# Top-k attention with a leaky-ReLU MLP on one core: earlier reciprocals, one TensorE transpose for each hurried pair of units, and a new chunk's MLP behind the exponentials

## The chip, the cores and the metric

The kernel runs on one core of a Trainium2 chip. A core has a matrix engine (TensorE, PE in the profile), a vector engine (VectorE, DVE), an engine for activations and copies (ScalarE, ACT), a general engine (GpSimd, POOL), a sync engine (SyncE, SP) that issues transfers, and 16 DMA engines. Each engine works through its own queue and waits for the others by semaphores. The metric is the time of one execution on the device in microseconds.

## The reference

What must be computed, cut to the core. Attention has 8 batches of 8 heads, 576 tokens and a head width of 64; the MLP works on the 4608 tokens at width 512, with 2048 hidden units.

```python
scores = scale * np.matmul(q, k.transpose(0, 1, 3, 2))
kth = np.partition(scores, -32, axis=-1)[..., -32:-31]
scores = np.where(scores >= kth, scores, -1000000000.0)
scores = scores - np.max(scores, axis=-1, keepdims=True)
attn = np.exp(scores)
attn = attn / (np.sum(attn, axis=-1, keepdims=True) + 1e-09)
attn_out = np.matmul(attn, v)
x = attn_out.transpose(0, 2, 1, 3).reshape(B * S, H * D)      # 4608 x 512
h = x @ w_in                                                   # 512 -> 2048
out = np.maximum(0.01 * h, h) @ w_out                          # 2048 -> 512
```

## The kernel before

**Units.** Attention is cut into 144 units. A unit holds 128 rows of queries of a pair of heads, so two score matrices of 128 x 576 (`both`). Where 64 rows are left over at the end of a sequence, a unit takes 64 rows of two pairs of heads. Four units in a row fill the width of 512 for their tokens.

**The steps of a unit.** `scores` multiplies queries and keys on TensorE for two units at once and ScalarE copies the result out of PSUM (L210, L217). `top_k` takes four rounds on VectorE: it first orders the two halves of each row into pairs (L240), then takes eight largest values (L245) and removes them (L248) in each of the four rounds. The first two rounds read 288 values, the last two 576. `mask` pushes all values below the 32nd down, on GpSimd (L258, L259). `exponents` and `sums` are on ScalarE (L262, L267): the result of `sums` is `ze`. `reciprocals` on VectorE makes `rz` of it (L271), and `normalize` multiplies with it on ScalarE (L274). Then the weights are transposed so that they can multiply the values (`weigh_values`, L318, on TensorE); `keep_values` copies the result into `x` of the chunk on ScalarE (L332).

**Two ways to transpose.** `transpose` splits the 32-bit words into two halves of 16 bits on ScalarE (L283), writes them to DRAM and has a DMA transposition read them back into `wT` (L286). `transpose_in_haste` does nine 128 x 128 transpositions on TensorE into two PSUM tiles named `wide` (L296) and copies these on ScalarE (L297). There are two `wide` tiles in all, and the scores and the weighted values use them too.

**Chunks.** The tokens are cut into 19 chunks: two of 128 and 17 of 256. A chunk's MLP can start when all of its units are weighted. `mlp` is a generator that does a few matmuls at each step: L343, L348, L353, L354 and L381 in the first two chunks, L369, L375 and L381 in the others; L388 copies the result out.

**The order.** It is written out by hand. There is one stage for each unit, and each engine gets its work in the order of the program. In stage s, VectorE does top k of unit s, GpSimd masks unit s-1, ScalarE exponentiates unit s-1, and unit s-2 is normalized and transposed. Every second stage computes the scores of two units ahead. `slot()` emits the next round of top k, and `mlp_steps(budget)` emits MLP matmuls, seven times in each stage; `slot_budget` spreads the backlog over the stages until the next chunk is complete.

**Hurried pairs.** `values_at` says in which stage a pair of units is weighted: the two units 2m and 2m+1 in stage 2m+4. Where the second of a pair completes one of the early chunks (units 3, 7, 15, 23 and 31: `HURRIED`), it is one stage earlier, at 2m+3, and both units of the pair are transposed on TensorE: the first at the end of stage 2m+2, the second at the start of stage 2m+3. There the reciprocals and the normalization come ahead of top k, and `values(s)` behind the first MLP slot. The chunk's MLP can then fill the six other slots of that stage.

Of the kernel before, what the change touches and what calls it, by code (L numbers as in the profile page):

```python
# [8 lines left out]
F32 = mybir.dt.float32  # L9
# [6 lines left out]
NKC = 5  # L16
# [3 lines left out]
def kernel(  # L20
# [14 lines left out]
    NPAIR, P, S = qT.shape  # L35
# [26 lines left out]
    work = ctx.enter_context(tc.tile_pool(name="work", bufs=2))  # L62
# [92 lines left out]
    def load_qk(pi):  # L155
        qt = loads.tile([P, S], F32, name="qt")
        kt = loads.tile([P, S], F32, name="kt")
        nc.sync.dma_start(qt, qT[pi])
        nc.sync.dma_start(kt, kT[pi])
        qk_of[pi] = qt, kt  # L160
# [108 lines left out]
    def reciprocals(u):  # L269
        u.rz = small.tile([P, 2], F32, name="rz")  # L270
        nc.vector.reciprocal(u.rz, u.ze)  # L271

    def normalize(u, i):
        nc.scalar.activation(u.s[i], u.s[i], AF.Copy, bias=0.0, scale=u.rz[:, i:i + 1])  # L274

    def transpose(u):


        pairs = u.both.rearrange("p i n -> p (i n)").bitcast(U16).rearrange("p (n h) -> p n h", h=2)
        apart = halves.tile([P, 2, 2 * S], U16, name="apart")  # L280
        for h in range(2):
            split = work.tile([P, 2 * S], U16, name="split", bufs=2)
            nc.scalar.copy(split, pairs[:, :, h])  # L283
            nc.sync.dma_start(apart[:, h, :], split)
        u.wT = work.tile([P, 2 * NKC - 1, P], F32, name="wT", bufs=3)
        nc.sync.dma_start_transpose(out=u.wT.bitcast(U16), in_=apart.rearrange("p h n -> (p h) n"))  # L286

    def transpose_in_haste(u):

        u.wT = work.tile([P, 2 * NKC - 1, P], F32, name="wT", bufs=3)  # L290
        both = u.both.rearrange("p i n -> p (i n)")
        for c0, c1 in ((0, 8), (8, 2 * NKC - 1)):
            pt = ps_sc.tile([P, 2, 512], F32, name="wide", bufs=2)
            pt = pt.rearrange("p h (c n) -> p (h c) n", n=P)
            for c in range(c0, c1):
                nc.tensor.transpose(pt[:, c - c0, :], both[:, c * P:(c + 1) * P], ident)  # L296
            nc.scalar.copy(u.wT[:, c0:c1, :], pt[:, 0:c1 - c0, :])  # L297


# [57 lines left out]
    def mlp(ch):  # L357

        n = CHUNKS[ch]
        t0 = sum(CHUNKS[:ch])  # L360
        x = x_of[ch]
        if ch < EARLY:
            yield from hidden_of_few(x)
        for f0 in range(0, NFC if ch >= EARLY else 0, 2):
            ph = ps_ml.tile([P, 2, CHMAX], F32, name="ph", tag="ml")
            for i in range(2):
                f = f0 + i
                for c in range(HP):
                    nc.tensor.matmul(  # L369
                        ph[:, i, 0:n], w_in[c][:, f * P:(f + 1) * P], x[c][:, 0:n],  # L370
                        start=(c == 0), stop=(c == HP - 1),
                    )
                    if c == 1 or i == 0 and c == HP - 1:
                        yield 2 * max(n, 225)
            nc.scalar.activation(gT[:, f0:f0 + 2, 0:n], ph[:, :, 0:n], AF.Prelu, alpha=SLOPE)  # L375
            yield 2 * max(n, 225)
        for r0 in range(0, n, P):
            m = min(P, n - r0)
            pz = ps_ml.tile([P, 512], F32, name="pz", tag="ml")
            for f in range(NFC):  # L380
                nc.tensor.matmul(  # L381
                    pz[0:m, 0:DMODEL], gT[:, f, r0:r0 + m], w_out[f // 4][:, f % 4, :],
                    start=(f == 0), stop=(f == NFC - 1),
                )
                if f % 2 and f + 1 < NFC:
                    yield 2 * DMODEL
            o_sb = work.tile([P, DMODEL], F32, name="o_sb", bufs=1)
            nc.scalar.copy(o_sb[0:m], pz[0:m, 0:DMODEL])  # L388
            nc.sync.dma_start(out[t0 + r0:t0 + r0 + m, :], o_sb[0:m])
            yield 2 * DMODEL  # L390
# [10 lines left out]
    def mlp_steps(budget):  # L401
        owed[0] += budget
        while owed[0] > 0:
            if running[0] is None:
                if not ready:
                    owed[0] = 0.0
                    return
                running[0] = mlp(ready.pop(0))
            cost = next(running[0], None)
            if cost is None:  # L410
                running[0] = None
            else:
                owed[0] -= cost
                backlog[0] -= cost
# [5 lines left out]
    HURRIED = {3, 7, 15, 23, 31}  # L420
# [24 lines left out]
    def slot_budget(s):  # L445

        after = [at for at, _ in ready_at if at >= s]
        until = after[0] if after else s
        few = len(after) >= len(CHUNKS) - EARLY
        return backlog[0] / (max(until + 1 - few - s, 1) * SLOTS)  # L450
# [3 lines left out]
    with tc.manual_schedule():  # L454
        last = {p: n for n, u in enumerate(steps) for p in u.pairs}

        def load_more(s):

            for of, load, n, lag in ((qk_of, load_qk, LOADED, -2), (v_of, load_v, LOADED_V, LAG + 1)):
                while len(of) < NPAIR and (len(of) < n or last[len(of) - n] + lag <= s):  # L460
                    load(len(of))


        for n in range(3):
            load_weights(n)
        rounding = {}
        for n in range(NPIECE + 2):
            for i in (n, n - 1, n - 2) if AS_WORDS else ():
                if 0 <= i < NPIECE:
                    if i == n:  # L470
                        rounding[i] = round_weights(i)
                    next(rounding[i], None)
            load_weights(n + 3)
            if 6 <= n < 6 + HP:
                load_qk(n - 6)
            elif n == NPIECE - 3:
                first_scores(steps[0])
            elif n == NPIECE:
                first_scores(steps[1])
            if n == NPIECE - 1:  # L480
                load_v(0)
                load_v(1)

        def values(s):
            due = [u for n, u in enumerate(steps) if values_at(n) == s]
            if due:
                po = ps_sc.tile([P, 2, 512], F32, name="wide", bufs=2)[:, 0, 0:2 * P]
                po = po.rearrange("p (u n) -> p u n", u=2)
            for part in (weigh_values, keep_values):
                for n, u in enumerate(due):  # L490
                    part(u, po[:, n, :])
            attended(s)

        for s in range(len(steps) + LAG + 1):
            cur, old, older, new = unit(s), unit(s - 1), unit(s - 2), ()
            if s % 2 == 0:
                new = [u for u in steps[s + 2:s + 4] if u]
            picks = top_k(cur) if cur else iter(())
            budget = slot_budget(s)

            def slot():
                next(picks, None)

            if s - 2 in HURRIED:
                reciprocals(older)
                normalize(older, 0)
                normalize(older, 1)
                transpose_in_haste(older)
                older = None
            slot()  # L510
            if old:
                mask(old, 0)
                mask(old, 1)
            mlp_steps(budget)
            if s - 2 in HURRIED:
                values(s)
                budget = slot_budget(s + 1)
            slot()
            if older:
                reciprocals(older)  # L520
                normalize(older, 0)
                normalize(older, 1)
            mlp_steps(budget)
            if old:
                exponents(old, 0)
            if older and s - 1 not in HURRIED:
                transpose(older)
            slot()
            mlp_steps(budget)
            mlp_steps(budget)  # L530
            slot()
            mlp_steps(budget)
            if old:
                exponents(old, 1)
                sums(old)
            if s - 1 in HURRIED:
                transpose_in_haste(older)
            if new and s < HURRY:
                scores(new)
            if s % 2 == 0:  # L540
                values(s)
            if new and s >= HURRY:
                scores(new)
            budget = slot_budget(s + 1)
            mlp_steps(budget)
            mlp_steps(budget)
            load_more(s)
        mlp_steps(1e9)
# [58 lines left out]
```

## Time and profile before

The median of three runs is 1501.92 us (1501.92 to 1502.21). The profiled execution spans 1500.9 us.

| Engine | Busy us | Share of the span | Main work |
|---|---|---|---|
| TensorE | 1405.3 | 94% | L381 509.5 us, L369 481.1 us |
| VectorE | 1328.8 | 89% | L245 635.6 us, L248 459.8 us, L240 213.7 us |
| ScalarE | 1091.2 | 73% | L283 293.8 us, L262 221.1 us, L274 207.0 us |
| GpSimd | 1097.8 | 73% | L258 638.3 us, L259 406.9 us |

A share of the span is an average: the first 75 us round the weights and load the first queries and keys, the last 55 us or so hold only the last chunk's MLP, and the stages in between are limited by different engines. A group of instructions has its line, its engine, the tile that it writes and those that it reads, its count, its busy time with the mean of one in ns, and the idle time of the engine just before it with what ended it. The chain of waits ran 31% of the span through L381, 26% through L369 and 10% through L318. The transpositions on TensorE are 90 instructions (L296), and the DMA transpositions 134.

### The profile page before, as it was taken

To read this page: it belongs to the slowest core of one execution; us is meant where nothing else is said; L and a number is where in the kernel's file an instruction comes from. 1 tells how busy PE (TensorE), PEld (TensorE's weight loads), DVE (VectorE), ACT (ScalarE), POOL (GpSimd) and SP (SyncE) were. 2 spreads that over 40 slices of the span, in tenths; PEclk is the share of its full clock that TensorE was granted. 3 is DMA by queue.
4 is the path that set the end of the run, shared out by engine and by line. 5 is a ranking of instruction groups with operands and counts; after the bars stand their busy time and mean duration, and the time that the engine had idled before them with its cause. 6 is when DMAs were issued, how large, how long until landed. Compare 5 with 4: busy or idle time off the path is not lost.

```text
span 1500.9 us, 24188 instructions
## 1 busy us (share of the span) xinstructions
PE 1405.3 (94%) x8122; PEld 934.6 (62%) x8122; DVE 1328.8 (89%) x3414; ACT 1091.2 (73%) x1979; POOL 1097.8 (73%) x742
## 2 busy tenths in 40 slices
PE   6709878999999999999999999999999999999999
PEld 2305446667575757575757676767676766666774
DVE  7997898979999999999999999999999999999600
ACT  8646676858688878787878787878787877777720
POOL 2286787868788887878878888777888888788700
PEclk9959989999999999999999999999999999999999
DMA  8621263624456455645664566555655555555510
GB/s 331 239 63 37 68 159 93 170 63 130 136 147 172 127 162 169 178 132 161 172 174 135 141 158 174 163 145 141 193 151 158 140 156 161 164 130 141 137 52 14
DMA packets 373053, 215.24 MB, mean 143 GB/s; under 512 B 319680, under 2 KB 319680, under 8 KB 370880
## 3 DMA queue, kind: packets, MB, share of 16 engines
q1 hardware_dynamic: 372928, 213.69, 50.5%
q8 instruction: 64, 1.05, 0.3%
q14 instruction: 61, 0.50, 0.1%
HBM read 46.14 MB, written 88.47 MB: 90 GB/s over the span
## 4 chain that ended last, share of the span: by engine, by line
PE 79%; DVE 8%; DMA 6%; ACT 5%; POOL 1%; issue 1%; SPq 0%; DVEq 0%; POOLq 0%; ACTq 0%
PE pz L381 31%; PE ph L369 26%; PE wide L318 10%; PE wide L210 6%; DMA wT<-apart 3%; PE narrow L210 3%; DVE tops L245 2%; DMA apart<-split 2%; ACT split L283 2%; DVE pairs L248 2%; ACT s_sb L274 1%; ACT s_sb L262 1%; PE ph L343 1%; ACT wT L297 1%; DVE w_out L149 1%
## 5 line engine op out<-in xcount | busy, mean ns | idle before, releaser
L258 POOL TENSOR_SCALAR pen<-s_sb,tops 128x576 f32<-128x576 f32 x288 | 638.3, 2216 | 233.6 <-DVE tops L245 201.9
L245 DVE MAX8 tops<-pairs 128x8 f32<-128x288 f32 (+1 forms) x1152 | 635.6, 591 | 0.0
L381 PE MATMUL pz<-w_out,gT 128*128 128x512 f32 x1152 | 509.5, 597 | 4.0 <-ACT gT L354 4.0
L369 PE MATMUL ph<-x,w_in 128*128 128x256 f32 x2176 | 481.1, 381 | 0.0
L248 DVE MATCH_REPLACE8 pairs<-tops,pairs 128x288 f32<-128x288 f32 (+1 forms) x864 | 459.8, 537 | 0.0
L369 PEld LDWEIGHTS ph<-x,w_in 128*128 128x128 f32 x2176 | 410.7, 190 | 77.1 <-issue 23.4
L259 POOL TENSOR_TENSOR s_sb<-s_sb,pen 128x576 f32<-128x576 f32 x288 | 406.9, 1413 | 24.0
L381 PEld LDWEIGHTS pz<-w_out,gT 128*128 128x128 f32 x1152 | 216.2, 190 | 271.0 <-issue 265.9
L283 ACT COPY split<-s_sb 128x1152 uint16<-128x1152 uint16 x268 | 293.8, 1145 | 0.0
L274 ACT ACTIVATE s_sb<-s_sb,rz 128x576 f32<-128x576 f32 x288 | 207.0, 769 | 38.9 <-DVE rz L271 38.8
L262 ACT ACTIVATE s_sb<-s_sb,nbias 128x576 f32<-128x576 f32 x288 | 221.1, 768 | 11.5 <-POOL s_sb L259 11.2
L240 DVE TENSOR_TENSOR pairs<-s_sb 128x576 f32<-128x576 f32 x288 | 213.7, 780 | 9.8
L318 PEld LDWEIGHTS wide<-wT,vt 128*64 128x64 f32 x3200 | 158.9, 138 | 57.3 <-ACT ze L267 17.4
L318 PE MATMUL wide<-wT,vt 128*64 128x128 f32 (+1 forms) x3200 | 178.1, 266 | 16.8 <-ACT wT L297 6.9
L375 ACT ACTIVATE gT<-ph 128x512 f32<-128x512 f32 x136 | 80.8, 594 | 79.4 <-PE ph L369 79.4
L332 ACT COPY x<-wide 128x128 f32<-128x128 f32 (+1 forms) x160 | 32.2, 260 | 142.2 <-PE wide L318 142.2
L217 ACT COPY s_sb<-wide 128x704 f32<-128x704 f32 x142 | 107.1, 754 | 24.3 <-PE wide L210 24.2
L210 PE MATMUL wide<-kt,qt 64*128 64x352 f32 (+1 forms) x632 | 117.1, 490 | 5.1 <-ACT wT L297 4.4
L271 DVE RECIPROCAL rz<-ze 128x2 f32<-128x2 f32 x144 | 22.4, 155 | 70.5 <-ACT ze L267 70.4
L217 ACT COPY s_sb<-narrow 128x448 f32<-128x448 f32 x142 | 68.7, 536 | 2.2 <-PE narrow L210 1.5
L388 ACT COPY o_sb<-pz 128x512 f32<-128x512 f32 x36 | 21.1, 586 | 64.1 <-PE pz L381 64.1
L210 PE MATMUL narrow<-kt,qt 64*128 64x224 f32 (+1 forms) x632 | 67.5, 358 | 0.0
(58 smaller groups left out, 596.1 us busy)
## 6 DMA issues: line engine op xcount, KB each, us to landing
apart<-split SPq DMA_DIRECT2D x268, 288.0 KB, 2.1
raw<-in_weights_dram SPq DMA_DIRECT2D x16, 1024.0 KB, 6.9
vt<-in_vk_dram SPq DMA_DIRECT2D x32, 320.0 KB, 3.5
qt<-in_qT_dram SPq DMA_DIRECT2D x32, 288.0 KB, 3.6
kt<-in_kT_dram SPq DMA_DIRECT2D x32, 288.0 KB, 3.9
out_dram<-o_sb SPq DMA_DIRECT2D x36, 256.0 KB, 2.0
wT<-apart SPq DMA_TRANSPOSE x134, 4.6
```

Of the source, the lines that this page charges most:

```text
L210: nc.tensor.matmul(to[r0:r0 + u.rows, i, :], qt[d, u.q0:u.q0 + u.rows], kt[d, k0:k1], start=True, stop=True)
L240: nc.vector.tensor_tensor(pairs[:, :, n, :], u.both[:, :, 0:HS], u.both[:, :, HS:S], op)
L245: nc.vector.max(out=u.tops[:, i, r, :], in_=rest[i])
L248: nc.vector.match_replace(out=rest[i], in_to_replace=u.tops[:, i, r, :], in_values=rest[i], imm_value=LOWEST)
L258: nc.gpsimd.tensor_scalar(pen, u.s[i], u.tops[:, i, ROUNDS - 1, 7:8], MASKED, ALU.is_lt, ALU.mult)
L259: nc.gpsimd.tensor_tensor(u.s[i], u.s[i], pen, ALU.add)
L262: nc.scalar.activation(u.s[i], u.s[i], AF.Exp, bias=u.nbias[:, i:i + 1], scale=SCALE, accum_out=u.z[:, i:i + 1])
L274: nc.scalar.activation(u.s[i], u.s[i], AF.Copy, bias=0.0, scale=u.rz[:, i:i + 1])
L283: nc.scalar.copy(split, pairs[:, :, h])
L318: nc.tensor.matmul(po[side * D:(side + 1) * D, o, :], vt[:, c, side, :], u.wT[:, c + side * NKC if c + 1 < NKC else c, r:r + n], start=(c ...
L369: nc.tensor.matmul(ph[:, i, 0:n], w_in[c][:, f * P:(f + 1) * P], x[c][:, 0:n], start=(c == 0), stop=(c == HP - 1),)
L381: nc.tensor.matmul(pz[0:m, 0:DMODEL], gT[:, f, r0:r0 + m], w_out[f // 4][:, f % 4, :], start=(f == 0), stop=(f == NFC - 1),)
```

## The change

Three things change in the order of a stage.

1. The reciprocals and the normalization of unit s-2 move from behind the second round of top k to behind the first, ahead of the first MLP slot. The hurried stages do them in the same place.
2. Of a hurried pair only the second unit is transposed on TensorE. The first goes the DMA way. `transpose_in_haste` is cut in two: the nine transpositions stand behind the second call of `slot()`, and the copies into `wT` (`keep_transposed`) behind the first exponential of unit s-1.
3. `values(s)` of a hurried stage moves to where it stands in all others, behind both exponentials and the sums. So a new chunk's MLP gets only the last two slots of that stage, and no longer stands ahead of these exponentials in ScalarE's queue.

In the changed file the lines behind `transpose_in_haste` are numbered five higher (L302 for the copies into `wT`, L323 for L318, L337 for L332, L374 for L369, L380 for L375, L386 for L381, L393 for L388).

```diff
--- before.py
+++ after.py
@@ -287,13 +287,18 @@
 
     def transpose_in_haste(u):
 
-        u.wT = work.tile([P, 2 * NKC - 1, P], F32, name="wT", bufs=3)
         both = u.both.rearrange("p i n -> p (i n)")
+        u.parts_T = []
         for c0, c1 in ((0, 8), (8, 2 * NKC - 1)):
             pt = ps_sc.tile([P, 2, 512], F32, name="wide", bufs=2)
             pt = pt.rearrange("p h (c n) -> p (h c) n", n=P)
             for c in range(c0, c1):
                 nc.tensor.transpose(pt[:, c - c0, :], both[:, c * P:(c + 1) * P], ident)
+            u.parts_T.append((c0, c1, pt))
+
+    def keep_transposed(u):
+        u.wT = work.tile([P, 2 * NKC - 1, P], F32, name="wT", bufs=3)
+        for c0, c1, pt in u.parts_T:
             nc.scalar.copy(u.wT[:, c0:c1, :], pt[:, 0:c1 - c0, :])
 
 
@@ -486,6 +491,8 @@
             if due:
                 po = ps_sc.tile([P, 2, 512], F32, name="wide", bufs=2)[:, 0, 0:2 * P]
                 po = po.rearrange("p (u n) -> p u n", u=2)
+            else:
+                return
             for part in (weigh_values, keep_values):
                 for n, u in enumerate(due):
                     part(u, po[:, n, :])
@@ -501,30 +508,23 @@
             def slot():
                 next(picks, None)
 
-            if s - 2 in HURRIED:
-                reciprocals(older)
-                normalize(older, 0)
-                normalize(older, 1)
-                transpose_in_haste(older)
-                older = None
             slot()
             if old:
                 mask(old, 0)
                 mask(old, 1)
-            mlp_steps(budget)
-            if s - 2 in HURRIED:
-                values(s)
-                budget = slot_budget(s + 1)
-            slot()
             if older:
                 reciprocals(older)
                 normalize(older, 0)
                 normalize(older, 1)
             mlp_steps(budget)
+            slot()
+            if s - 2 in HURRIED:
+                transpose_in_haste(older)
+            mlp_steps(budget)
             if old:
                 exponents(old, 0)
-            if older and s - 1 not in HURRIED:
-                transpose(older)
+            if older:
+                keep_transposed(older) if s - 2 in HURRIED else transpose(older)
             slot()
             mlp_steps(budget)
             mlp_steps(budget)
@@ -533,12 +533,9 @@
             if old:
                 exponents(old, 1)
                 sums(old)
-            if s - 1 in HURRIED:
-                transpose_in_haste(older)
             if new and s < HURRY:
                 scores(new)
-            if s % 2 == 0:
-                values(s)
+            values(s)
             if new and s >= HURRY:
                 scores(new)
             budget = slot_budget(s + 1)
```

## The prediction

> **What bounds the kernel now.** I read the page first for the busy shares and their slices, then busy time by stretches, then the gaps in TensorE's timeline, and last the reciprocals in VectorE's timeline. The page:
>
> ```profile
> PE 1405.3 (94%) x8122; PEld 934.6 (62%) x8122; DVE 1328.8 (89%) x3414; ACT 1091.2 (73%) x1979; POOL 1097.8 (73%) x742
> ...
> PE   6709878999999999999999999999999999999999
> ```
>
> TensorE is the bound, but not from the start: the low digits are the second to the eighth slice (37.5 us each). Busy time by stretches, cut where the MLPs of chunk 0, 1 and 2 begin (125.2, 171.5, 247.0):
>
> ```profile
> 125.20:171.50 46.30, 42.09 (x213) 23.02 (x212) 36.03 (x95) 29.90 (x60) 32.68 (x22) 1.00 0.19 52
> 171.50:247.00 75.50, 58.68 (x356) 32.85 (x354) 70.52 (x184) 54.59 (x102) 58.98 (x41) 0.91 0.48 133
> 247.00:450.00 203.00, 196.13 (x1213) 139.92 (x1212) 187.20 (x488) 152.65 (x293) 157.83 (x106) 1.00 0.45 124
> 450.00:1442.00 992.00, 988.90 (x5867) 670.74 (x5866) 922.33 (x2399) 769.50 (x1413) 787.40 (x526) 1.00 0.57 154
> ```
>
> The first busy column is TensorE, the third VectorE. TensorE idles 16.8 us between 171.5 and 247, where VectorE is 93% busy, then 6.9 us up to 450, then 3.1 us in 992. So from 247 on each microsecond of TensorE work or idleness counts in full; before 247 the question is when chunk 2 can begin, and there VectorE's top k and what ScalarE feeds it set the pace. The gaps of a hurried pair, and VectorE's longest stalls:
>
> ```profile
> 109.24 2.18 PE L296 MATMUL wide<-ident,s_sb 128*128 128x128 f32 x9 [36.12 <-ACT s_sb L274]
> 112.75 1.54 PE L210 MATMUL wide<-kt,qt 64*128 64x352 f32 x4 [1.33 <-ACT wT L297]
> ...
> 120.44 1.43 PE L296 MATMUL wide<-ident,s_sb 128*128 128x128 f32 x9 [1.21 <-ACT s_sb L274]
> 122.86 2.40 PE L318 MATMUL wide<-wT,vt 128*64 128x128 f32 x40 [0.99 <-ACT wT L297]
> ```
>
> ```profile
> 133.99 0.17 DVE L271 RECIPROCAL rz<-ze 128x2 f32<-128x2 f32 x1 [8.01 <-ACT ze L267]
> ...
> 173.27 0.17 DVE L271 RECIPROCAL rz<-ze 128x2 f32<-128x2 f32 x1 [3.79 <-ACT ze L267]
> ...
> 249.31 0.17 DVE L271 RECIPROCAL rz<-ze 128x2 f32<-128x2 f32 x1 [3.39 <-ACT ze L267]
> ```
>
> Each hurried unit makes TensorE wait about 1 us before its transposes or after them. Each stall of VectorE stands just behind the beginning of a chunk's MLP (125.2, 171.5, 247.0): ScalarE works in order, and the exponentials of the stage stand behind the new chunk's L348 or L375.
>
> **What the Trainium skill says.** "PSUM — Partial Sum Buffer", Engine vs sequencer instructions: ScalarE's and VectorE's queues are strict FIFO. The trace agrees: ze at 133.75 came behind two L348, and rz 8.01 us late. "TensorE: Matmul & The Clock Gate", Part 4: a transpose on TensorE lands in PSUM and needs a copy after it. Here that copy (L297, 1.02 us) is the 0.99 us wait of L318. Same page, "HAM oscillation — how this bites in real kernels": long idle gaps bring the array back to half rate. The trace agrees: nine transposes took 2.18 us behind a gap of 36.12 us and 1.15 us elsewhere. "Perfetto Trace Analysis", Optimization Strategy: a kernel may have several regimes with different most-contended engines; this one changes over at 247.
>
> **The change, part by part.**
>
> Fewer transposes. Five even units (2, 6, 14, 22, 30) go back to the DMA way: 45 transposes and 10 L297 copies go; ten L283 (1.05 us each) come on ScalarE, with five more DMA transposes. From the end of L283 to values that way takes 2.1 + 4.6 + 0.4 = 7.1 us by the chain of waits; in stage 16 L283 should end near 227.5, wT land at 234.6, and its values start at 237: hidden, by 2.5 us. In the saturated part (units 22, 23, 30, 31) a unit costs 2.13 to 2.42 us from transposes to values now, in all 8.8 us. Afterwards two units remain, with MLP steps between transposes and values, so only some 1.05 us of issue each: saving 6.7 us.
>
> Reciprocals earlier. A round of top k at 288 wide is 1.57 us (two MAX8 at 0.36, two MATCH_REPLACE8 with their loads at 0.43). rz asks for ze that much earlier in VectorE's order; queued behind it are rounds 2 to 4, hence tops, GpSimd's masks and the exponentials one stage on. In the saturated part rz waits for ze anyway in every second stage, so masks come 1.57 us later against TensorE. Their slack there: the second mask ended at 622.0 and its exponential started at 624.8, so 1.2 us are left of 2.8 us and nothing waits. Normalize moves ahead of the first MLP slot: wT lands some 1 us sooner, against the remaining DMA waits of TensorE (0.5 to 1.3 us, 5.8 us in all). I take 2 us back, with bounds of 0 and 5.
>
> The hurried stages. Here I laid the new order by hand along the durations that the trace of before shows: top k stage 8.87; after a waiting rz 1.57 + 4.29 to the next stage; masks ready 3.15 and 6.95 after the stage's start; normalize 1.35, exponential 0.75 to 0.9, two L283 2.1, scores 2.35, values 2.35, L343 0.89 and L381 0.87 per instruction, wT copy 1.06.
> Stage 5: transposes of unit 3 at 118.3 (rz at 115.5, ScalarE free at 117.5), wT copied at 120.7 (behind one exponential), values 5 at 120.6 to 123.0. Chunk 0 begins at 123.0, against 125.2.
> VectorE no longer stalls 8.01 us; it now waits for ze of unit 5 at 135.1 (1.9 us), of unit 6 at 146.6 (2.8 us, behind L283, since TensorE's L381 also waits 2.7 us for a gT copy that now stands behind it). Stage 8 starts at 140.9 (now 147.2), stage 10 at 161.4 (now 164.9).
> Stage 9: ScalarE normalizes unit 7 after the x copies at 162.5; transposes 163.2 to 164.6 (1.2 us of idleness), two L381 to 166.5, then the wT copy behind o_sb and an exponential, 168.7 (2.2 us of idleness), values to 171.0. Chunk 1 begins at 171.0, against 171.5: no gain. ze of unit 8 stands behind that, at 169.9: rz waits 5.6 us, and stage 11 starts at 175.8 (now 177.6).
> Then VectorE runs nearly without waits: stage 14 at 202.4, stage 15 at 211.3 (now 204.2 and 214.7; the 1.60 us stall of 210.4 goes, since normalize leaves the way of ze), stage 17 at 229.0 (now 232.4). In stage 17: masks at 232.2 and 236.0, o_sb and normalize to 235.4 or 236.9, transposes to 236.2 or 237.6, wT at 237.1 or 238.6, values to 239.5 or 241.0, the second figures with TensorE at half rate during values 16. Chunk 2 begins at 240.3, against 247.0. Today the way there is longer, because mask 15, a wT copy, scores, values 16 and a second set of transposes stand one behind the other.
> GpSimd does the same masks as before. Added time on the DMA queue is nothing beside the 7.1 us above.
>
> Sum: before, 1500.9 - 247.0 = 1253.9 us follow the start of chunk 2. Of it 6.7 and 2 go: 1245.2. 240.3 + 1245.2 = 1485.5 us of span; the time was 1.0 above the span, so 1486.5 us. VectorE doesn't become the bound: 126 stages from 237.9 at 8.9 end at 1359, while the last reciprocal starts at 1421.0 now.
>
> **The rivals.** A: the start is won but not kept, or chunk 1's late start drags on. The mechanism would be the stall of 5.6 us found above and one like it in stage 17. For it: ze still stands behind wT copies and o_sb. Against: from stage 11 on no chunk begins until 17. Then chunk 2 begins near 245 and the rest gives 1245.2: 1491 us. B: the start is won in full, half-rate values don't happen and DMA waits vanish: chunk 2 at 236, rest 1242, 1479 us. C, slower: rz one round earlier stalls VectorE in every pair of stages by 1.57 us, masks turn up late, and exponentials hold back the MLP's L375 in the saturated part. For it: VectorE waited for ze 59 times already, 70.4 us. Against: the slack of 1.2 us and more above. If a third of 63 pairs lost 1.57 us each to TensorE, 33 us would be lost and 15 won: 1520 us. A milder C, with new waits in hurried stages that eat up all gain of the start and of the transposes, ends at 1502.
>
> **How the numbers follow.** Forecast 0.50, A 0.22, B 0.15, C with its milder form 0.13. The predicted time is that of the forecast, 1486.5. The range runs from B less 3 us for a full use of the DMA waits (1476) to A plus most of a milder C (1498), and leaves out C beyond it, and the tail below. Faster by over 0.2% (below 1498.9): 0.50 + 0.22 + 0.15 = 0.87, and C splits into 0.04 within 0.2% and 0.09 slower.
>
> **What would show it.** Right: 45 transposes left; MLP of chunk 0 at about 123, of chunk 1 at 171, of chunk 2 at 240; VectorE's stalls at rz of 2, 3 and 6 us instead of 8.0 and 3.8; TensorE with at most 4 us of idleness from chunk 2 to the last values; the last chunk's MLP still some 55 us. Wrong: exponentials waiting for GpSimd's masks after 450; a wait of L318 for wT by DMA in stages 5, 9 or 17; TensorE's idleness after 450 above 5 us; chunk 2 not before 247.

## The result and the profile after

The changed kernel took 1496.05 us (median of four runs, 1494.76 to 1496.35) against 1502.07 us of the kernel before (median of four, 1501.92 to 1505.69). The ratio of the means is 0.9953, with a 95% interval of 0.9935 to 0.997; the medians give 0.9960. It is faster by 6.0 us; 15.4 us were forecast. The profiled execution spans 1494.4 us, against 1500.9.

First the page of the changed kernel, with the lines that were shown of before:

```profile
PE 1405.4 (94%) x8075; PEld 934.0 (63%) x8077; DVE 1328.8 (89%) x3414; ACT 1095.0 (73%) x1979; POOL 1096.5 (73%) x742
...
PE   6718887999999999999999999999999999999999
```

TensorE's busy time has not fallen (1405.3 before), although 45 transposes are gone. The low slices are the second to the seventh, in the kernel before too: the fourth and the seventh have lost a tenth, the third and the sixth have won one. Busy time by stretches of the changed kernel, cut again where the MLPs of chunk 0, 1 and 2 begin (now 124.6, 174.6, 250.2); the first busy column is TensorE, and behind the five engines stands TensorE's granted clock:

```profile
124.60:174.60 50.00, 42.76 (x204) 22.30 (x202) 36.48 (x96) 29.90 (x57) 33.79 (x24) 0.97 0.27 77
174.60:250.20 75.60, 59.66 (x347) 33.57 (x345) 72.18 (x189) 56.21 (x105) 59.87 (x40) 0.86 0.52 145
250.20:450.00 199.80, 198.56 (x1208) 139.97 (x1207) 189.89 (x492) 157.25 (x296) 159.07 (x106) 1.00 0.53 145
450.00:1440.00 990.00, 988.28 (x5875) 672.62 (x5874) 918.21 (x2393) 766.02 (x1406) 783.65 (x524) 1.00 0.57 153
```

Chunk 2 begins at 250.2, which is 3.2 us later than before (247.0). The gain is made behind it: 1494.4 - 250.2 = 1244.2 us, against 1253.9. There TensorE idles 1.2 and 1.7 us in the two stretches, in place of 6.9 and 3.1. The clock of the first two stretches is 0.97 and 0.86; it was 1.00 and 0.91.

TensorE around the values (L318 before, L323 now) and behind its longer gaps, first in the kernel before, then in the changed one. Each line has the start, the length, the instruction, and in brackets the idle time ahead of it with what ended it:

```profile
115.57 1.32 PE L210 MATMUL wide<-kt,qt 64*128 64x352 f32 x4
116.83 2.40 PE L318 MATMUL wide<-wT,vt 128*64 128x128 f32 x40
...
236.55 2.40 PE L318 MATMUL wide<-wT,vt 128*64 128x128 f32 x40
...
244.64 2.40 PE L318 MATMUL wide<-wT,vt 128*64 128x128 f32 x40 [0.99 <-ACT wT L297]
```

```profile
98.00 1.39 PE L210 MATMUL wide<-kt,qt 64*128 64x352 f32 x4
112.89 4.35 PE L323 MATMUL wide<-wT,vt 128*64 128x128 f32 x40 [13.51 <-ACT s_sb L217]
118.45 1.43 PE L296 MATMUL wide<-ident,s_sb 128*128 128x128 f32 x9 [1.21 <-ACT s_sb L274]
120.87 3.79 PE L323 MATMUL wide<-wT,vt 128*64 128x128 f32 x40 [0.99 <-ACT wT L302]
...
147.11 13.98 PE L386 MATMUL pz<-w_out,gT 128*128 128x512 f32 x28 [2.68 <-ACT gT L359]
...
234.48 0.64 PE L210 MATMUL narrow<-kt,qt 64*64 64x224 f32 x2 [6.00 <-DMA kt<-in_kT_dram]
...
236.59 3.94 PE L323 MATMUL wide<-wT,vt 128*64 128x128 f32 x40
...
246.22 4.07 PE L323 MATMUL wide<-wT,vt 128*64 128x128 f32 x40 [0.99 <-ACT wT L302]
```

Forty matmuls of the values took 2.40 us before in stages 4, 5, 16 and 17; now they take 4.35, 3.79, 3.94 and 4.07. TensorE's granted clock in the values of stages 4 and 5 was 1.00 and is now 0.53 and 0.62. Ahead of 234.48 TensorE waits 6.00 us for keys that haven't been loaded. And VectorE's waits at rz in the changed kernel, up to the start of chunk 2:

```profile
136.72 0.17 DVE L271 RECIPROCAL rz<-ze 128x2 f32<-128x2 f32 x1 [3.33 <-ACT ze L267]
...
148.58 0.17 DVE L271 RECIPROCAL rz<-ze 128x2 f32<-128x2 f32 x1 [2.90 <-ACT ze L267]
...
173.41 0.17 DVE L271 RECIPROCAL rz<-ze 128x2 f32<-128x2 f32 x1 [7.01 <-ACT ze L267]
...
209.84 0.17 DVE L271 RECIPROCAL rz<-ze 128x2 f32<-128x2 f32 x1 [0.88 <-ACT ze L267]
```

The 8.01 us stall of before was at rz of unit 4, in stage 6. That rz doesn't wait any more, but the two after it wait 3.33 and 2.90 us, and rz of unit 8 in stage 10 waits 7.01 us in place of 3.79. Up to the start of chunk 2 the stalls at rz add up to 14.1 us, against 13.4 before: they have moved, not gone.

### The profile page after: what moved, and what is told of

Read it like the earlier page. It is cut to its first block, busy times and chain, and to the rows that moved or that the text cites. A ratio compares the mean times of both kernels' runs of the same rounds, so it can differ in the third digit from the quotient of the medians.

```text
span 1494.4 us, 24122 instructions
## 1 busy us (share of the span) xinstructions
PE 1405.4 (94%) x8075; PEld 934.0 (63%) x8077; DVE 1328.8 (89%) x3414; ACT 1095.0 (73%) x1979; POOL 1096.5 (73%) x742
## 4 chain that ended last, share of the span: by engine, by line
PE 86%; DVE 7%; ACT 3%; DMA 3%; issue 1%; SPq 0%; POOL 0%; DVEq 0%; ACTq 0%
PE pz L386 34%; PE ph L374 30%; PE wide L323 11%; PE wide L210 6%; PE narrow L210 3%; DVE tops L245 2%; DVE pairs L248 1%; DMA wT<-apart 1%; PE ph L348 1%; ACT split L283 1%; DMA apart<-split 1%; ACT s_sb L262 1%; DVE w_out L149 1%; DVE w_in L149 1%; DVE scale L146 1%
## 5 line engine op out<-in xcount | busy, mean ns | idle before, releaser
L386 PE MATMUL pz<-w_out,gT 128*128 128x512 f32 x1152 | 511.5, 599 | 5.4 <-ACT gT L359 5.4
L374 PE MATMUL ph<-x,w_in 128*128 128x256 f32 x2176 | 481.1, 381 | 0.0
L374 PEld LDWEIGHTS ph<-x,w_in 128*128 128x128 f32 x2176 | 410.7, 190 | 77.1 <-issue 23.4
L386 PEld LDWEIGHTS pz<-w_out,gT 128*128 128x128 f32 x1152 | 216.6, 191 | 272.7 <-issue 266.0
L283 ACT COPY split<-s_sb 128x1152 uint16<-128x1152 uint16 x278 | 304.8, 1145 | 0.0
L323 PEld LDWEIGHTS wide<-wT,vt 128*64 128x64 f32 x3200 | 164.1, 141 | 64.0 <-ACT ze L267 17.4
L323 PE MATMUL wide<-wT,vt 128*64 128x128 f32 (+1 forms) x3200 | 182.8, 271 | 20.8 <-ACT s_sb L217 13.5
L337 ACT COPY x<-wide 128x128 f32<-128x128 f32 (+1 forms) x160 | 32.2, 261 | 150.0 <-PE wide L323 150.0
L380 ACT ACTIVATE gT<-ph 128x512 f32<-128x512 f32 x136 | 80.7, 593 | 74.8 <-PE ph L374 74.7
L210 PEld LDWEIGHTS wide<-kt,qt 64*128 64x128 f32 (+1 forms) x632 | 48.5, 178 | 40.1 <-ACT s_sb L217 22.5
```

Of the source, the lines that this page charges most:

```text
L210: nc.tensor.matmul(to[r0:r0 + u.rows, i, :], qt[d, u.q0:u.q0 + u.rows], kt[d, k0:k1], start=True, stop=True)
L323: nc.tensor.matmul(po[side * D:(side + 1) * D, o, :], vt[:, c, side, :], u.wT[:, c + side * NKC if c + 1 < NKC else c, r:r + n], start=(c ...
L374: nc.tensor.matmul(ph[:, i, 0:n], w_in[c][:, f * P:(f + 1) * P], x[c][:, 0:n], start=(c == 0), stop=(c == HP - 1),)
L386: nc.tensor.matmul(pz[0:m, 0:DMODEL], gT[:, f, r0:r0 + m], w_out[f // 4][:, f % 4, :], start=(f == 0), stop=(f == NFC - 1),)
```

## The experiments

Four theories were set against one another. Theory 1: the change does what it was meant to, and the start of chunk 2 came 9.9 us later than reckoned because TensorE ran at half rate (a granted clock near 0.5) and waited for a load of keys. Theory 2: the earlier reciprocals cost VectorE time and eat the gain. Theory 3: masks, exponentials or another wait stand right behind these losses, so that removing them gains nothing. Theory 4: the later values cost TensorE more than VectorE's stalls did. Each edit is to the changed kernel, save the first.

| Experiment | Median us | Ratio to before, 95% interval | Chunk 2 begins | Span behind it |
|---|---|---|---|---|
| the change | 1496.05 | 0.9953 (0.9935 to 0.997) | 250.2 | 1244.2 |
| recips only | 1504.34 | 1.0014 (1.0006 to 1.0021) | 253.5 | 1254.0 |
| recips undone | 1498.84 | 0.9979 (0.9969 to 0.9989) | 253.1 | 1244.2 |
| all loads early | 1503.29 | 1.0002 (0.9993 to 1.0011) | 247.7 | 1256.2 |
| warm stage 4 | 1493.28 | 0.9937 (0.9925 to 0.9949) | 247.4 | 1245.3 |
| one load early | 1492.46 | 0.9932 (0.9917 to 0.9947) | 248.7 | 1243.1 |
| load and warm | 1488.67 | 0.991 (0.9896 to 0.9925) | 241.3 | 1244.5 |
| split later | 1499.95 | 0.998 (0.9973 to 0.9987) | 247.0 | 1251.2 |
| values early | 1498.71 | 0.9971 (0.9962 to 0.998) | 250.4 | 1247.2 |
| both on TensorE | 1500.03 | 0.9985 (0.9978 to 0.9992) | 250.8 | 1245.6 |
| best | 1486.04 | 0.9893 (0.9878 to 0.9908) | 238.4 | 1245.3 |

The last two columns are of one profiled execution each, in which the values of stage 4 already begin up to 1.1 us apart for the same work; the median is over 4 to 22 runs, which differ by up to 7.6 us in one kernel. So an edit is read by where its profile moves, and its size by the median. Each ratio is to runs of the kernel before that were made beside it; their medians are 1502.88 to 1503.02 us in the experiments, against 1502.07 beside the change, so a difference of medians between two rows is good to about 1 us. The intervals of recips undone, warm stage 4, one load early and values early overlap with that of the change; for these four the place in the profile has to carry the argument.

**Reciprocals only.** In the kernel before:

```diff
+            if older:
+                reciprocals(older)
+                normalize(older, 0)
+                normalize(older, 1)
             mlp_steps(budget)
             if s - 2 in HURRIED:
                 values(s)
                 budget = slot_budget(s + 1)
             slot()
-            if older:
-                reciprocals(older)
-                normalize(older, 0)
-                normalize(older, 1)
             mlp_steps(budget)
```

> The kernel before with the reciprocals and normalization of the usual stages behind the first round of top k, and nothing else of the change. Theory 1 (ze, not rz's place, sets the pace; the change lost its gain elsewhere): VectorE stalls longer at rz but at the same instants, chunk 2 begins at 247 within 1 us, wT lands earlier, so TensorE's small DMA waits (5.8 us in all) shrink by 2 to 4 us: 1498 to 1502 us. Theory 2 (the earlier reciprocal costs VectorE 1.57 us in many stages and eats the gain): slower than before, 1504 us or more.

1504.34 us, which is theory 2's figure; the ratio's interval lies just above 1. In the profile chunk 2 began at 253.5, not within 1 us of 247 as theory 1 had it: with the values still ahead of the exponentials, VectorE waits 10.25 us for ze in stage 6 (8.01 before) and 7.12 us in stage 18 (3.39 before). That execution was the second longest of the 22, 5 us above the median, so its 6.5 us overstate the usual loss. So the first part alone is no gain: where ze is late, asking for it one round sooner makes the wait longer. Of theory 2 the figure holds, not the mechanism: behind chunk 2 the time is 1254.0 us, against 1253.9 before, so the earlier reciprocals cost nothing in the many stages there.

**Reciprocals undone.** In the changed kernel:

```diff
-            if older:
-                reciprocals(older)
-                normalize(older, 0)
-                normalize(older, 1)
             mlp_steps(budget)
             slot()
+            if older:
+                reciprocals(older)
+                normalize(older, 0)
+                normalize(older, 1)
             if s - 2 in HURRIED:
```

> The changed kernel with reciprocals and normalization back behind the second round of top k. Theory 1: the first stages lose a little, since normalize stands behind a slot of the MLP again, and DMA waits return: 1496 to 1501 us. Theory 2: VectorE gets its 1.57 us back and the kernel is faster than the changed one: 1488 to 1493 us.

1498.84 us, 2.8 us slower by the medians, as theory 1 has it and theory 2 doesn't. In the profile it all lies in the start (253.1 in place of 250.2); the time behind chunk 2 is 1244.2 with or without. So the first part, no gain alone, is worth something together with the others. TensorE's waits for DMA behind chunk 2 are 3.4 us without it and 2.9 with it, against 5.8 in the kernel before: their fall is mostly not its doing.

**All loads early.**

Queries and keys of a freed buffer are loaded one stage sooner:

```diff
-  ... last[len(of) - n] + lag <= s):
+  ... (last[len(of) - n] // 2 * 2 if lag < 0 else last[len(of) - n]) + lag <= s):
```

> The changed kernel with the queries and keys of a freed buffer loaded one stage sooner, where both units of the pair of units have had their scores. Theory 1: the wait of 6.0 us of L210 for kt in stage 16 goes; the values of that stage then wait for ScalarE's first copy of scores at 233.7 in place of 236.6, so chunk 2 begins 2.9 us earlier: 1493.2 us (1491.5 to 1494.5). Theory 3 (another wait stands right behind it, so the load costs nothing): 1495.5 to 1496.5 us.

1503.29 us: a miss by 10 us. Chunk 2 did begin 2.5 us earlier, but 12 us were lost behind it. SyncE's queue in this experiment shows one of the places:

```profile
550.95 0.38 SPq L158 DMA_DIRECT2D qt<-in_qT_dram  x1
...
554.46 0.43 SPq L159 DMA_DIRECT2D kt<-in_kT_dram  x1
554.98 1.21 SPq L284 DMA_DIRECT2D apart<-split  x2
561.87 2.73 SPq L286 DMA_TRANSPOSE wT<-apart  x1
```

And TensorE behind it, in the same experiment, and the same matmuls in the changed kernel:

```profile
566.64 1.31 PE L323 MATMUL wide<-wT,vt 128*64 128x128 f32 x20 [3.44 <-DMA wT<-apart]
```

```profile
566.29 1.31 PE L323 MATMUL wide<-wT,vt 128*64 128x128 f32 x20 [0.44 <-DMA wT<-apart]
```

Eight loads now follow one another from 550.95 to 554.9, ahead of a unit's two halves, and the DMA transposition begins 6.9 us behind the first half's issue. In the changed kernel behind chunk 2 that distance is 3.3 us where no load stands ahead (median of 89) and 5.4 us behind four loads (median of 6, the longest 7.0). In this experiment the three longest waits for wT (3.58, 3.44 and 1.72 us) stand behind six, eight and four loads in a row; after another eight, from 888.3, the wait is 0.70 us only. TensorE idles 11.7 us behind chunk 2, up to 1450; in the changed kernel it is 3.0. Whether the loads delay the halves in the queue or by the bandwidth they take isn't shown.

**Warm stage 4.** Two matmuls whose result is not used, as soon as unit 3's first exponential is done:

```diff
+            if s in {4}:
+                pd = ps_ml.tile([P, 512], F32, name="pd", tag="ml")
+                for _ in range(2):
+                    nc.tensor.matmul(pd, ident, old.s[0][:, 0:512], start=True, stop=True)
             values(s)
```

> The changed kernel with two matmuls of 128x512 on TensorE ahead of the values of stage 4, whose result is not used, as soon as unit 3's first exponential is done. Theory 1 (TensorE at half rate costs the start of chunk 0): the clock is full when the values begin at 112.9; the values of stage 4 and 5 take 2.4 us each in place of 4.35 and 3.79, chunk 0 begins near 121.3 in place of 124.6, and chunk 2 some 3 us earlier: 1493 us (1491.5 to 1494.5). Theory 3 (masks and exponentials set the pace of the start anyway): 1495.5 to 1496.5 us.

1493.28 us, within 0.3 us of theory 1's. Chunk 0 begins at 121.9 and chunk 2 at 247.4. TensorE's timeline of this experiment, in which L541 are the idle matmuls (the two show as four records):

```profile
109.39 3.78 PE L541 MATMUL pd<-s_sb,ident 128*128 128x512 f32 x4 [9.77 <-ACT s_sb L262]
113.12 2.77 PE L323 MATMUL wide<-wT,vt 128*64 128x128 f32 x40
...
119.52 2.40 PE L323 MATMUL wide<-wT,vt 128*64 128x128 f32 x40 [0.99 <-ACT wT L302]
```

The granted clock is 0.50 in the idle matmuls, 0.85 in the values of stage 4 and 1.00 in those of stage 5. It is 2.8 us for added work that computes nothing: the cost was the clock. The five runs (1491.5 to 1494.46) all lie below the four of the change (1494.76 to 1496.35).

**One load early.** Only pair 7, whose keys unit 19 needs in stage 16:

```diff
-  ... last[len(of) - n] + lag <= s):
+  ... last[len(of) - n] + lag - (lag < 0 and len(of) == 7) <= s):
```

> The changed kernel with one pair of heads' queries and keys (the pair that unit 19's scores in stage 16 need) loaded one stage sooner, and all other loads as they were. Loading all of them sooner brought chunk 2 forward to 247.7, but TensorE then idled 11.7 us instead of 3.0 behind it, since eight loads in a row stood ahead of a later unit's halves and DMA transposition in the sync engine's queue. Theory 1 (the kt wait costs the start 2.9 us, the loads' order in the queue did the rest): chunk 2 begins at 247.3 within 0.7, TensorE's idleness after it stays near 3 us, 1493 us (1491 to 1494.5). Theory 3 (a start won by loading earlier is lost again): 1496 us or more.

1492.46 us, and no wait for kt is left. Values of stage 16 then wait 4.67 us for ScalarE's first copy of scores, so the load's worth is less than the 6.00 us that are gone. Chunk 2 began at 248.7, later than the 247.3 within 0.7 that was expected, because this execution was already 1.3 us late at the start of chunk 1; from there to chunk 2 it took 72.8 us in place of 75.6, so 2.8 us less. By the medians it is 3.6 us, and 2.9 were expected.

**Load and warm.** Both edits, with the idle matmuls in stages 4 and 16.

> The one early load, and two matmuls of 128x512 without use ahead of the values of stage 4 and of stage 16. Theory 1 (half rate and the load make up the gap between the forecast 240.3 and the measured 250.2 of chunk 2's start): values of stages 4, 5, 16 and 17 take 2.4 us each, chunk 2 begins 2.9 + 3.2 + 3.2 us earlier, at 241 within 1.5, and the rest stays 1244: 1487 us (1485 to 1489.5). Theory 3: the pieces hide one another, 1492 us or more.

1488.67 us, chunk 2 at 241.3; both within what was expected. TensorE's timeline of this experiment, against the one of the changed kernel above:

```profile
119.51 2.40 PE L323 MATMUL wide<-wT,vt 128*64 128x128 f32 x40 [0.99 <-ACT wT L302]
...
227.13 1.98 PE L541 MATMUL pd<-s_sb,ident 128*128 128x512 f32 x4 [0.93 <-ACT s_sb L262]
230.87 2.40 PE L323 MATMUL wide<-wT,vt 128*64 128x128 f32 x40 [1.75 <-ACT s_sb L217]
...
238.96 2.40 PE L323 MATMUL wide<-wT,vt 128*64 128x128 f32 x40 [0.99 <-ACT wT L302]
```

The values are back at 2.40 us where they stood at 3.79, 3.94 and 4.07; those of stage 4 take 2.73. Theory 3 falls for these two losses.

**Split later.** The usual units' halves behind the third MLP slot:

```diff
-            if older:
-                keep_transposed(older) if s - 2 in HURRIED else transpose(older)
+            if s - 2 in HURRIED:
+                keep_transposed(older)
             slot()
             mlp_steps(budget)
+            if older and s - 2 not in HURRIED:
+                transpose(older)
             mlp_steps(budget)
```

> The changed kernel with the usual units' halves (L283) and DMA transposition behind the third MLP slot of a stage rather than behind the first exponential, so that chunk 0 and 1 get their gT copies ahead of them on ScalarE. Theory 1: L386's waits of 2.68 us for gT go, and with them the half rate behind them (13.98 us for 28 matmul records in place of 12.1), so chunk 1 begins some 3 us earlier; wT comes up to 1 us later in the saturated part: 1492 to 1496 us. Theory 3 (masks set the pace there): 1496 to 1499 us.

1499.95 us, slower than was expected. The start gained what it should: chunk 0's L386 waits 0.57 us for gT in place of 2.68 and takes 12.28 us in place of 13.98, chunk 1 begins at 170.9 in place of 174.6, and chunk 2 at 247.0. But wT comes too late in the saturated part (behind the start of chunk 2, where TensorE hardly idles): TensorE's waits for its DMA add up to 9.3 us there, against 2.9.

**Values early.** The third part undone:

```diff
+            if s - 2 in HURRIED:
+                keep_transposed(older)
+                values(s)
+                budget = slot_budget(s + 1)
             if old:
                 exponents(old, 0)
-            if older:
-                keep_transposed(older) if s - 2 in HURRIED else transpose(older)
+            if older and s - 2 not in HURRIED:
+                transpose(older)
...
-            values(s)
+            if s - 2 not in HURRIED:
+                values(s)
```

> The changed kernel with the third part undone: in hurried stages the copies into wT and the values stand ahead of the first exponential again, and the new chunk's MLP gets the slots behind them. Theory 1 (that part is worth its stalls): ze comes later behind the new chunk's L353 and L380, VectorE stalls 8 us or more at rz of unit 4 and in stages 10 and 18 again, and chunk 2 begins 2 to 5 us later than 250.2: 1498 to 1502 us. Theory 4 (a chunk's start half a stage sooner is worth more to TensorE than VectorE's stalls cost): 1488 to 1494 us.

1498.71 us, 2.7 us slower by the medians. VectorE's waits for ze are 5.88 us in stage 6 and 6.68 us in stage 18, where the changed kernel has none in stage 6 and 1.98 us in stage 18. Of theory 1's figures the time came true, but none of the stalls reached 8 us, and the one in stage 10 is shorter than in the changed kernel (5.22 us, against 7.01). The stalls up to chunk 2 add up to 13.5 us, against 14.1. So the third part moves the stalls of VectorE and hardly lessens them. The start of chunk 2 hardly moved, although this execution was 1.1 us late at the values of stage 4, and 3.0 us are lost behind it, of which 1.8 us are longer waits of TensorE for DMA and for ScalarE's copies of x. Theory 4 falls.

**Both on TensorE.** The second part undone:

```diff
-            if older:
+            if older and s - 1 not in HURRIED:
                 keep_transposed(older) if s - 2 in HURRIED else transpose(older)
...
                 sums(old)
+            if s - 1 in HURRIED:
+                transpose_in_haste(older)
+                keep_transposed(older)
```

> The changed kernel with the second part undone: the first unit of a hurried pair is transposed on TensorE again at the end of its stage, ahead of the scores, and its wT copied at once. Theory 1 (that part is worth 2.1 to 2.4 us for each of two units in the saturated part, by the chain of before): 45 transposes more, the time behind the start of chunk 2 goes from 1244.2 to 1248 to 1250; the transposes of stage 4 and 16 bring TensorE's clock up ahead of the values there, so chunk 2 begins at 249 within 3: 1496 to 1502 us. Theory 3 (the transposes are hidden): the time behind chunk 2 stays at 1244.

1500.03 us, 4.0 us slower by the medians. In the profiled execution only 1.4 us of it lie behind chunk 2, less than the 4 to 6 expected; that execution took 1498.19 us, the shortest of the 20. Behind chunk 2 its trace does have the cost that theory 1 named: 36 transposes (4.6 us) in place of 18 (2.3 us), and 2.0 us of waits for wT copies, which the changed kernel doesn't have. So the transposes aren't hidden there, as theory 3 had it; but 1.2 us of waits for DMA are gone in return, and the net size stays open. TensorE's timeline of the start shows one thing more:

```profile
115.70 1.35 PE L210 MATMUL wide<-kt,qt 64*128 64x352 f32 x4
116.98 2.41 PE L323 MATMUL wide<-wT,vt 128*64 128x128 f32 x40
```

The values of stage 4 take 2.41 us here. As in the kernel before, the scores have waited behind the transposes (112.88, 112.75 before) and run up to the values without a gap. In the changed kernel the same scores are over by 99.4, and the values begin after 13.51 us of idleness. The second part had taken away the delay that put work right ahead of the values.

**The best version.** Load and warm, and the halves behind the third slot in stages up to the seventh only (`s < 8`).

> The one early load, the two idle matmuls ahead of the values of stages 4 and 16, and the halves of the usual units behind the third MLP slot in the stages up to the seventh alone. Theory 1 (each of the three losses is the start's own, and the later halves cost DMA waits only where TensorE is saturated): chunk 1 begins 3 us earlier than with the load and the clock alone (171.9), chunk 2 at 238.3 within 1.5, and the rest stays 1244 to 1245: 1485.5 us (1483.5 to 1487.5). Theory 3 (the masks hold chunk 1 back): 1488 to 1490 us.

1486.04 us, faster than both kernels: 0.9893 of before (0.9878 to 0.9908). Chunk 2 begins at 238.4. Whether it beats load and warm alone isn't settled by the times, since the intervals overlap; in the profile chunk 1 begins at 168.5 in place of 171.9.

## Why the prediction fell short

The direction held, and the time lies within the range, but the gain is 6.0 us where 15.4 were forecast. The sum had two terms: the time behind the start of chunk 2, which came out right, and the start of chunk 2, which failed.

- **Behind chunk 2: right.** 1245.2 us were reckoned, 1244.2 measured. The parts can be seen in the two traces. TensorE waited 4.0 us for wT copies before and doesn't now, and the transposes there take 2.3 us in place of 4.9: together 6.6 us, with 6.7 reckoned. Its waits for DMA fell from 5.8 to 2.9 us, with 2 reckoned; but that was put down to the earlier normalization, and undoing the first part left the 1244.2 unchanged, and that part alone left the waits at 5.7 us. So this figure was right by luck; what shortened the waits isn't shown. The parts undone one at a time don't give the sum back: 0, 1.4 and 3.0 us in their profiles.
- **The slack of the masks: right.** 1.2 us were to be left, and in the changed kernel a second mask ended at 617.8 and its exponential started at 619.0. Exponentials waited 1.1 us for masks in all behind 450.
- **"Chunk 0 begins at 123.0": 1.6 us short, and chunk 1 3.6 us.** TensorE's half rate was seen in the trace of before and applied to values 16 only, as one of two ends. It also struck values 4 (4.35 us), values 5 (3.79 us) and the first L386 behind the gT wait (13.98 us for 28 records; 12.27 before). The values and the L386 that delayed chunk 1 took 1.4 and 1.7 us more than at full rate. The prediction counted the transposes as work removed, and not what their going does to the work behind them: the scores of stage 4 moved up from 112.8 to 95.2 and left TensorE idle ahead of the values. Warm stage 4, and both on TensorE, show it.
- **"Chunk 2 begins at 240.3": 9.9 us short, the step that failed.** The hand-laid order put TensorE's half rate at nothing everywhere but in values 16, and the wait for keys in stage 16 at nothing. 3.5 us came along from chunk 1 through VectorE; 0.9 us is the stall at 209.84, reckoned at nothing. Stage 17 so began at 233.4 in place of 229.0. The scores of stage 16 were taken as ready when TensorE is free, and they waited for kt. Its load was issued at 229.8 in the changed kernel and at 230.4 in the kernel before, so it isn't later than it was; before, the scores stood behind a wT copy (their first matmul came at 232.7, in place of 226.9), and TensorE did not wait for the keys. A wait that had been hidden came to light when the work ahead of it left. Its net worth by the starts is 236.6 - 233.7 = 2.9 us. Values 16 and 17 at half rate took 1.5 and 1.7 us more than 2.4, of which 0.7 was in the forecast. 3.5 + 0.9 + 2.9 + 2.5 = 9.8 us. With the load and the clock of the values mended chunk 2 began at 241.3, a microsecond from the forecast. That it comes so close is in part chance: chunk 0 began 1.1 us sooner there than forecast, and the slow L386 was still in; with that mended too (best) it is 238.4.
- **The stalls of VectorE.** Forecast 1.9, 2.8 and 5.6 us; measured 3.33, 2.90 and 7.01. Their places were right. The first is longer by about as much as chunk 0 was late. At the last, ze came 3.5 us later than forecast, with chunk 1, and VectorE got there 2.1 us later.
- **The rivals.** A (the start won but not kept, 1491 us) came nearest in time, 5 us off, but its chance of 0.22 rested on stalls of VectorE and not on the two causes that were there. C's first step, the earlier reciprocal, is a loss in the kernel before and a gain in the changed one.
- **The signs.** Of the signs of being wrong, one came: chunk 2 did not begin before 247. The others stayed away, but for the 1.1 us of exponentials that waited for masks; TensorE's idleness after 450, up to 1440, was 1.7 us.
- **Two readings of before.** The low digits end with the seventh slice, not the eighth. And nine transposes took 1.15 us in four places and 1.43 us in five, so "1.15 us elsewhere" is the shorter of two usual figures. Neither enters the sum.

## What to carry to other kernels

When a change takes work away ahead of a wait, ask what that work was hiding: a load that was just in time, or a clock that was up because something ran right ahead. A start that is laid out by hand must be laid out for every resource that the next step reads, the loads and their queue among them, and at both clock rates. And a part of a change can't be judged alone: here each part costs 2.7 to 4.0 us by the medians when it is undone, give or take 1, and the first without the others loses.

## What the runs showed of the hardware

Two matmuls without use ahead of a burst shortened the whole kernel by 2.8 us. After the gap of 13.5 us ahead of stage 4 the values took 4.18 to 4.54 us in all six profiles without these matmuls or the transposes ahead (the change, recips undone, all loads early, one load early, split later, values early). For shorter gaps the outcome varied. One sequence, nine transposes, four records of L386 in 1.88 us, a gap of 2.34 us and then values, gave 2.40 us for the values in the changed kernel (172.26) and 4.05 us in both on TensorE (174.92). So the clock's fall is not a matter of gap length alone.

Another place shows the same. Between the last matmul that is no transpose and the values of stage 17 lay 3.8 us in the kernel before (240.9 to 244.6) and in the changed one (242.4 to 246.2), with nine transposes in them both times; the values took 2.40 us before and 4.07 us after. The Trainium skill's "TensorE: Matmul & The Clock Gate", Part 4, says that transposes don't count as busy in the same way, and its section "What's actually happening" that the window in which activity is judged runs freely; both fit these figures, and no run here tests either by itself. A gap of 2.68 us ahead of L386, with 1.3 us of transposes ahead of it, was followed by 13.98 us for 28 records; a gap of 0.57 us, by 12.28 us.
